# A recurrent attention block and a SoLU feed-forward block on one core: the slot's work put in order of TensorE's tile form

## The chip, the cores and the metric

One core of a Trainium2 chip runs the whole program. The time is that of one execution on the device, in microseconds; for the kernel before, three runs gave 583.88, 577.79 and 580.46, median 580.46. TensorE (PE) multiplies matrices, VectorE (DVE), ScalarE (ACT) and GpSimd (POOL) work elementwise, SyncE (SP) issues transfers. Each takes its own instructions in order. TensorE writes only to PSUM, which here is split into four pairs of banks, named A, B, C and h; whatever stands in a pair must be read out before the next product goes there.

## The reference

For four batches and eight heads of width 40, over 768 tokens, a state S (40 by 40) is carried along; all is float32:

```
y[t] = r[t] . S
Sa   = S . a[t]
S    = S * w[t] - outer(Sa, b[t]) + outer(v[t], k[t])
```

The outputs of the heads, side by side, are x, 3072 tokens of 320. The weights w_in (320 by 1024) and w_out (1024 by 320) come as float64. The second block is

```
h    = x @ w_in
solu = h * softmax(h)
ln   = (solu - mean) / sqrt(var + 1e-6) * g
out  = ln @ w_out
```

## The kernel before

**Tiling.** A chunk is 64 tokens of two batches, so there are 24 chunks (i = 0 to 23), and chunk i carries on the state that chunk i-2 left. Within a chunk the recurrence is written as products of 64 by 64: logs of w are added up by a triangular product (`decay`, L337: pcum), the exponentials scale a, b, k, and r. Everything is transposed on TensorE with an identity (`turned`, L358: a, b, ei, k, v, r and the state) and copied out. `norm` (L424) forms the products of a and b; their lower triangles, 32 by 32, go to DRAM (nt_dram), come back for two chunks at once as blk, one matrix to a partition, and `invert` (L456) inverts them on VectorE in 30 steps of two instructions each (prod, uu; L469 and L471). The inverse goes to DRAM (uu_dram) and `bring` (L481) loads it as tu and uh. `flip` (L494) transposes tu on VectorE; `couple` (py) and `close` (pz) build the 64 by 64 inverse from the parts; a copy by ScalarE follows each (wy, nt, tu).

**A chunk's path.** `scores` (L571) gives ps, masked by VectorE to psi and lv; `carried` and `driven` (L589, L605) add up px from the state and from psi, which ScalarE copies as x0; `solved` (L617) gives pu, out of which come lu's two parts; `read` (L632) gives pyo; `leave` (L646) adds the state's share on VectorE (tot), multiplies on GpSimd by the decays to x and the next state, and SP and POOL queues move x to xT; `stated` and `stated_r` (L551, L559) turn the state and read it with r (pst, psr).

**The second block.** `hidden` (L689) multiplies xT by w_in: contraction 320 = 128 + 128 + 64, the last part with 64-row tiles; `highest`, `exped`, `weighed`, `spreadof` (L701 to L737) are maximum on VectorE, exponential on ScalarE, product on VectorE, square and its sum on ScalarE (written into h's PSUM pair, as a place to throw it), and a power on GpSimd. `folded` (L739) transposes the result to lnT, `output` (L752) multiplies by w_out in two halves of four, and ScalarE scales and copies to osb.

**Weights.** The float64 words are loaded in 13 parts (`land`, L156) and made float32 ("narrowing", `split`, L180) by VectorE and ScalarE in three pieces, begun, scaled and finished. When a part is finished, the next part's load may be issued on the POOL queue.

**Order.** The loop at L863 runs over slots i = -1 to 27, and the order in which calls stand there is the order on every engine; nothing is moved by a scheduler. With LAG = 1, a slot does the recurrence of chunk i, prepares a, b and decays of chunk i+5 and k, v, r of chunk i+2, runs softmax and layer norm of chunk i-3 and the output of chunk i-4. A string for each slot (`plans`, L853) says at six places how many inverse steps VectorE takes there (a number) and where a part of the weights is begun, scaled or finished (b, s, f). From slot 5 on there are two strings, for odd and even slots.

Of the kernel before, what the change touches and what calls it, by code (L numbers as in the profile page):

```python
# [24 lines left out]
LAG = 1  # L25
# [25 lines left out]
def kernel(  # L51
# [32 lines left out]
    small = ctx.enter_context(tc.tile_pool(name="small", bufs=3))  # L84
# [33 lines left out]
    a_t = zeroed(nc.vector, "a", [P, H, C], 4, pad)  # L118
    ei_t = zeroed(nc.vector, "ei", [P, H, C], 1, pad)
    ex_t = [const.tile([P, 2, 4, C + 1], FP32, name=f"ex{n}") for n in range(AHEAD + 2)]  # L120
# [102 lines left out]
    def vector(plan, kept=0):  # L223

        for word in plan.split():
            if word in "bsf":
                dict(b=begin_narrow, s=scale_narrow, f=end_narrow)[word]()
            else:
                some(int(word), kept)

    def turn_g():
        pg = pair("B", "pg")[:, 0]
        nc.tensor.transpose(out=pg[:, 0:NF], in_=g_rows, identity=ident[0:NF, 0:NF])
        for x, y in zip(g_cols, (0, -20, -36)):
            nc.scalar.mul(out=x, in_=pg[:, 0:NF], mul=2.0 ** y)
# [6 lines left out]
    def mean_of(lo, hi, begun, tag):  # L242
        t = pair(tag, "pmean")[:, 0]
        nc.tensor.matmul(t[:, 0:DM], lhsT=ident, rhs=begun, start=True, stop=False)
        mean_part(t, lo, hi, False)
        return mean_kept(t)
# [59 lines left out]
    def load_keys(i, names, queue=nc.sync):  # L306
        if not ok(i):
            return
        for n, ap in (("w", w), ("b", b), ("a", a), ("k", k)):
            if n in names:  # L310
                x = a_t[i % 4] if n == "a" else two.tile([P, H, D], FP32, tag="raw_" + n, name="raw_" + n,
                                                             bufs=3)
# [3 lines left out]
    def load_values(i):  # L316
# [4 lines left out]
        d["raw_r"] = two.tile([P, H, D], FP32, tag="raw_r", name="raw_r")  # L321
        load(d["lv"][:, :, C:], v, i)
        load(d["raw_r"], r, i, nc.gpsimd)
# [13 lines left out]
    def decay(i):  # L337
        if not ok(i):
            return
# [3 lines left out]
        t = (pair("B", "pcum")[:, 0] if i > 9 else h_pair("pcum"))[:, 0:DM]  # L343
        nc.tensor.matmul(t, lhsT=c_("cum"), rhs=d["lw"], start=True, stop=True)  # L344
        nc.scalar.activation(out=ei_t[0][:, :, 0:D], in_=heads(t), func=AF.Exp)
        inv = d["inv"] = two.tile([P, DM], FP32, tag="inv", name="inv", bufs=4)
        nc.scalar.activation(out=inv, in_=t, func=AF.Exp, scale=-1.0)  # L347
# [28 lines left out]
    def decay_turned(i, t=None, y=0):  # L376
# [3 lines left out]
        ex = st[i]["ex"] = ex_t[i % (AHEAD + 2)]  # L380
# [37 lines left out]
    def shared_pair(i):  # L418

        if i not in shared:  # L420
            shared[i] = pair("A", "py")
        return shared[i]

    def norm(i, first=lambda: None):  # L424
# [15 lines left out]
        queue = nc.sync if 1 < i < 4 else nc.gpsimd  # L440
        for x in range(2):
            for e in range(2):
                home = C * x + Q * e
                queue.dma_start(out=blocks[n][e].rearrange("(a x h) s c -> a x s h c", a=GRP, x=2)[at, x],  # L444
# [68 lines left out]
    def close(i):  # L513
# [3 lines left out]
        t = pair("B" if i < 4 else "A", "pz")  # L517
        for u in in_turn(lambda p, q, g, h: (p, p ^ h)):
            p, q, g, h = u
            j = 2 * q + g  # L520
            mm(t[half(p ^ h), p, j * Q:j * Q + Q], wy[half(p), h, j], d["uh"][half(p), H * (p ^ h) + 4 * p + j])
        nc.scalar.copy(out=d["tu"].rearrange("p (h j) c -> p h j c", h=2)[:, :, :, 2 * Q:],
                       in_=t[:, :, 0:4 * Q].rearrange("p h (j c) -> p h j c", j=4))
# [14 lines left out]
    def attend_r(i, tag):  # L538
        if not ok(i):
            return lambda: None  # L540
        t = turned(pair(tag, "pr"), 0, r_t[0])
# [17 lines left out]
    def stated_r(i):  # L559
# [4 lines left out]
        t = pair("C", "psr")  # L564
# [6 lines left out]
    def scores(i):  # L571
# [3 lines left out]
        t = pair("B", "ps")  # L575
# [13 lines left out]
    def carried(i):  # L589
# [5 lines left out]
        d["px"] = pair("C", "px")  # L595
# [9 lines left out]
    def driven(i):  # L605
        if not ok(i):
            return
# [7 lines left out]
        nc.scalar.mul(out=x0, in_=d["px"].rearrange("p h (j d) -> p h j d", j=4)[:, :, :, 0:W2], mul=-1.0)  # L615

    def solved(i):  # L617

        if not ok(i):
            return  # L620
# [9 lines left out]
        nc.scalar.copy(out=o[:, :, :, C:], in_=y[:, :, :, C:])  # L630
# [15 lines left out]
    def leave(i):  # L646
        if not ok(i):
            return
# [9 lines left out]
        else:  # L658
            nc.vector.tensor_copy(out=by_b(tot), in_=y)
        x = two.tile([P, 4, P], FP32, tag="x", name="x", bufs=1)  # L660
        ex = d["ex"][0:W2]
        by_q = lambda x, q: x[0:W2, q::2].rearrange("p (b g) c -> p b g c", b=2)
        for q in range(2):
            nc.gpsimd.tensor_tensor(out=x[0:W2, 2 * q:2 * q + 2].rearrange("p g (b t) -> p b g t", b=2),  # L664
                                    in0=by_q(tot, q)[:, :, :, 0:C], in1=ex[:, :, 2 * q:2 * q + 2, 0:C], op=ALU.mult)
        d["x"] = x
        xT = d["xT"] = two.tile([P, NK, P], FP32, tag="xT", name="xT", bufs=3)
# [3 lines left out]
        if ci == NCH - 1:  # L671
            return
        for q in range(2):
            nc.gpsimd.tensor_tensor(out=by_q(state_of(i)[:, 1], q)[:, :, :, 0:D], in0=by_q(tot, q)[:, :, :, C:],
                                    in1=ex[:, :, 2 * q:2 * q + 2, C:].to_broadcast([W2, 2, 2, D]), op=ALU.mult)
# [13 lines left out]
    def hidden(i, some):  # L689
# [4 lines left out]
        for kt, x in some:  # L694
            if (kt, x) == (0, 0):
                d["h"] = h_pair("h")
            part = slice(0, P) if kt < 2 else half(x)
            mm(d["h"][:, 512 * x:512 * x + 512], d["xT"][part, kt], w_in[part, 2 * kt + (x if kt < 2 else 0)],
               start=(kt, x) in ((0, 0), (NK - 1, 1)), stop=(kt, x) in ((NK - 1, 0), (1, 1)))
# [25 lines left out]
    def spreadof(i):  # L725
# [9 lines left out]
        nc.scalar.activation(out=d["h"], in_=d["e"], func=AF.Square, scale=-float(DFF), bias=d["mu"], accum_out=sq)  # L735
# [3 lines left out]
    def folded(i):  # L739
# [4 lines left out]
        t = pair("A", "plnT")  # L744
# [7 lines left out]
    def output(i, x):  # L752
# [4 lines left out]
        if x == 0:  # L757
            d["out"] = pair("B", "po")[:, 0, 0:DM]
        t = d["out"]
        for f in range(x * NF // 2, x * NF // 2 + NF // 2):  # L760
            nc.tensor.matmul(t, lhsT=d["lnT"][:, f, :], rhs=w2[:, f, :], start=f == 0, stop=f == NF - 1)  # L761
        if x == 0:
            return
# [9 lines left out]
    def some(n, kept=0):  # L773
        while len(steps) > kept and n:
            if next(steps[0], steps) is steps:
# [6 lines left out]
    def begin_inverse(n):  # L782
        steps.append(invert(n))
        next(steps[-1])
# [11 lines left out]
    decay(0)  # L796
    logged(1)
    decay_turned(0)()
    for i in range(4):
# [6 lines left out]
        decay(i + 1)  # L806
# [6 lines left out]
        if i == 1:  # L813
# [8 lines left out]
            load_values(0)  # L822
            load_keys(1, "k")
# [144 lines left out]
```

## Time and profile before

| | before |
|---|---|
| runs, us | 577.79, 580.46, 583.88 |
| span of the profiled execution, us | 580.2 |
| PE, PE weight load busy | 510.6 (88%), 360.5 (62%) |
| DVE, ACT, POOL busy | 407.9 (70%), 316.9 (55%), 299.8 (52%) |
| granted TensorE clock, mean | 0.93 |
| start of pu of chunk 0, 5, 6, 18, 23 | 63.7, 179.4, 199.0, 434.8, 529.2 |
| the chain that ended last | PE 65%, DVE 17%, DMA 9% |

The profile is of one execution, whose own time is its span; it lies 0.2 us under the median. Busy shares are means over stages that have different bounds, so the stages are read by themselves. A product of float32 appears as two instructions. The length that a row gives for a TensorE group contains the time that the last product needs to come out, during which the next group already runs; the distance from one group's start to the next start is what it costs. pu's start marks a slot's beginning in the order before; after the change pu stands late in its slot, and by then the output of chunk i-4, the rest of h, and transposes of this slot have been done, about 8.5 us of TensorE that come later before the change.

### The profile page before, as it was taken

How to read it: one execution, taken by the hardware profiler on the slowest of the kernel's cores; microseconds unless marked ns; L12 is line 12 of the kernel's file. 1: busy time of each engine (PE TensorE's matmuls, PEld its weight loads, DVE VectorE, ACT ScalarE, POOL GpSimd, SP SyncE). 2: the span in 40 equal slices, each digit the busy share in tenths (PEclk: the TensorE clock that was granted, in tenths of full speed). 3: DMA queues.
4: the chain of work that ended last, by engine and by line, in shares of the span. 5: the costliest groups of instructions: out<-in, count | busy, mean ns of one | idle time of the engine just before them, and what ended most of it. 6: DMA issues, size and time to landing. Idle time of an engine off the chain costs nothing.

```text
span 580.2 us, 25261 instructions
## 1 busy us (share of the span) xinstructions
PE 510.6 (88%) x10773; PEld 360.5 (62%) x10773; DVE 407.9 (70%) x1072; ACT 316.9 (55%) x618; POOL 299.8 (52%) x534
## 2 busy tenths in 40 slices
PE   4462764876989999999999999999999989999995
PEld 3241653654766777677667767777777657666543
DVE  4698986996894886877959869779688487332121
ACT  4633573755646565756566566656564455444533
POOL 4554484555635736648576467475773554233200
PEclk9656787879779999999999999999999989999999
DMA  7896886746605536637555475365431431311110
GB/s 152 151 155 135 175 183 114 148 94 113 112 16 124 111 74 134 118 63 141 103 104 114 90 143 113 65 137 105 99 77 39 106 74 32 62 33 27 27 24 23
DMA packets 188200, 56.71 MB, mean 98 GB/s; under 512 B 171680, under 2 KB 181512, under 8 KB 188088
## 3 DMA queue, kind: packets, MB, share of 16 engines
q1 hardware_dynamic: 173288, 36.98, 34.6%
q0 software_dynamic: 12368, 17.19, 12.9%
q8 instruction: 85, 1.39, 1.0%
q10 hardware_dynamic: 2432, 0.92, 0.8%
q14 instruction: 27, 0.22, 0.1%
HBM read 40.10 MB, written 10.22 MB: 87 GB/s over the span
## 4 chain that ended last, share of the span: by engine, by line
PE 65%; DVE 17%; DMA 9%; issue 3%; ACT 3%; SPq 2%; POOL 1%; ACTq 0%; DVEq 0%; POOLq 0%
PE h L276 19%; PE po L761 15%; PE px L276 5%; DVE uu L471 5%; DVE prod L469 5%; PE pyo L276 4%; DMA uu_dram<-uu 3%; PE py L276 3%; PE ps L276 3%; PE pu L276 3%; PE pz L276 2%; PE pkv L363 2%; DMA tu<-uu_dram 2%; PE plnT L747 2%; PE psr L276 2%
## 5 line engine op out<-in xcount | busy, mean ns | idle before, releaser
L276 PE MATMUL h<-w_in,xT 128*128 128x512 f32 (+1 forms) x288 | 123.6, 632 | 0.3
L761 PE MATMUL po<-w,lnT 128*128 128x320 f32 x384 | 118.2, 454 | 1.8 <-ACT lnT L750 1.8
L471 DVE TENSOR_TENSOR uu<-uu,prod 128x30 f32<-128x30 f32 (+4 forms) x360 | 106.2, 295 | 12.4
L469 DVE TENSOR_TENSOR prod<-blk,uu 128x30 f32<-128x30 f32 (+4 forms) x360 | 105.5, 293 | 11.4 <-POOL kb L356 0.7
L664 POOL TENSOR_TENSOR x<-tot,ex 104x256 f32<-104x256 f32 x48 | 32.3, 690 | 130.3 <-DVE tot L656 119.5
L761 PEld LDWEIGHTS po<-w,lnT 128*128 128x128 f32 x384 | 71.3, 194 | 31.9 <-issue 3.2
L444 POOL DMA_DIRECT2D nt_dram<-nt x88 | 52.3, 602 | 24.3 <-ACT c L734 21.4
L276 PEld LDWEIGHTS h<-w_in,xT 128*128 128x128 f32 (+1 forms) x288 | 40.4, 190 | 34.3 <-issue 29.1
L706 DVE TENSOR_REDUCE nmax<-h 128x1 f32<-128x1024 f32 x24 | 29.4, 1224 | 38.0 <-PE h L276 37.5
L510 ACT ACTIVATE wy<-py,cst 128x256 f32<-128x256 f32 x24 | 11.4, 474 | 79.0 <-PE py L276 79.0
L403 DVE TENSOR_TENSOR lu<-pu,cst 128x512 f32<-128x512 f32 x24 | 16.5, 688 | 51.6 <-PE pu L276 51.6
L686 POOL DMA_DIRECT2D xT<-x x96 | 48.7, 511 | 1.2 <-DMA blk<-nt_dram 1.2
L276 PE MATMUL py<-tu,nt 64*64 64x32 f32 x768 | 16.5, 226 | 28.0 <-DVE tot L656 11.6
L714 ACT ACTIVATE e<-h,nmax 128x1024 f32<-128x1024 f32 x24 | 26.8, 1117 | 20.4 <-DVE nmax L706 20.3
L299 POOL DMA_DIRECT2D raw_r<-in_r_dram x48 | 33.8, 707 | 1.4 <-issue 1.3
L276 PEld LDWEIGHTS py<-tu,nt 64*64 64x64 f32 x768 | 15.6, 145 | 30.3 <-issue 19.8
L344 PE MATMUL pcum<-lw,cst 128*128 128x320 f32 x48 | 21.7, 538 | 14.4 <-ACT lw L335 14.4
L737 POOL TENSOR_TENSOR rs<-var,mhalf 128x1 f32<-128x1 f32 x24 | 13.6, 567 | 39.5 <-ACT var L736 38.8
L356 POOL TENSOR_TENSOR kb<-raw_b,inv 128x320 f32<-128x320 f32 x24 | 21.1, 880 | 21.1 <-ACT inv L347 6.9
L722 DVE SCALAR_TENSOR_TENSOR e<-h,e 128x1024 f32<-128x1024 f32 x24 | 29.2, 1215 | 3.8 <-ACT e L714 3.8
L276 PEld LDWEIGHTS pu<-x,tu 64*64 64x64 f32 x768 | 19.5, 142 | 16.8 <-ACT kvT L536 13.7
L735 ACT ACTIVATE h<-e,mu 128x1024 f32<-128x1024 f32 x24 | 26.8, 1116 | 4.1 <-DVE e L722 4.1
(131 smaller groups left out, 1068.9 us busy)
## 6 DMA issues: line engine op xcount, KB each, us to landing
blk<-nt_dram POOLq DMA_DIRECT2D x22, 256.0 KB, 3.7
raw_w<-in_w_dram SPq DMA_DIRECT2D x48, 80.0 KB
a<-in_a_dram SPq DMA_DIRECT2D x48, 80.0 KB
raw_r<-in_r_dram POOLq DMA_DIRECT2D x48, 80.0 KB, 3.5
lv<-in_v_dram SPq DMA_DIRECT2D x48, 80.0 KB
out_dram<-osb SPq DMA_DIRECT2D x47, 80.0 KB
raw_b<-in_b_dram SPq DMA_DIRECT2D x44, 80.0 KB
raw_k<-in_k_dram SPq DMA_DIRECT2D x42, 80.0 KB
```

Source lines behind the costliest of these rows:

```text
L276: nc.tensor.matmul(o, lhsT=lhsT, rhs=rhs, start=start, stop=stop, skip_group_check=True)
L299: queue.dma_start(out=x[half(p), :, 0:D], in_=ap[2 * bp + p, :, ci * C:(ci + 1) * C, :].rearrange("h t d -> t h d"))
L444: queue.dma_start(out=blocks[n][e].rearrange("(a x h) s c -> a x s h c", a=GRP, x=2)[at, x], in_=nt[home:home + Q].rearrange("p h j c -> p ...
L469: nc.vector.tensor_tensor(out=t, in0=nb[:, j:j + 1, j + 1:Q].to_broadcast([P, n_c, m]), in1=u[:, 0:n_c, j:j + 1].to_broadcast([P, n_c, m]) ...
L471: nc.vector.tensor_tensor(out=u[:, 0:n_c, j + 1:Q], in0=u[:, 0:n_c, j + 1:Q], in1=t, op=ALU.subtract)
L664: nc.gpsimd.tensor_tensor(out=x[0:W2, 2 * q:2 * q + 2].rearrange("p g (b t) -> p b g t", b=2), in0=by_q(tot, q)[:, :, :, 0:C], in1=ex[:, : ...
L686: nc.gpsimd.dma_start(out=xT[to:to + Q, 2], in_=x[at + P - 3 * D:at + D, 2])
L706: nc.vector.tensor_reduce(out=nmax, in_=d["h"], axis=AX.X, op=ALU.max, negate=True)
L714: nc.scalar.activation(out=e, in_=d["h"], func=AF.Exp, bias=d["nmax"], accum_out=d["esum"])
L722: nc.vector.scalar_tensor_tensor(out=d["e"], in0=d["h"], scalar=1.0 / DFF, in1=d["e"], op0=ALU.mult, op1=ALU.mult, accum_out=d["mu"])
L735: nc.scalar.activation(out=d["h"], in_=d["e"], func=AF.Square, scale=-float(DFF), bias=d["mu"], accum_out=sq)
L761: nc.tensor.matmul(t, lhsT=d["lnT"][:, f, :], rhs=w2[:, f, :], start=f == 0, stop=f == NF - 1)
```

## The change

- **TensorE's order.** A slot now begins with all transposes (ei, b, k, v in pairs C and B; a and r in pair A), h's 64-row products, lnT's and the state's transposes; then h's 128-row products, the decay sum and the output, unbroken; then pu, psr, ps, px from the state, py (both), pyo, pz, px from psi. k, v and r are turned for chunk i+1, not i+2, and the scores of chunk 0 go from the prologue to slot -1.
- **PSUM.** h is in pair C, psr, px, lnT's transposes and the thrown-away square in pair h, ps in C, po, py and pz in B. All eight output products stand in one place.
- **Evictions** of px (x0) and the leaving of chunk i (state first, then x) are done at the start of slot i+1; lu's copy comes after psr's.
- **x and state** are multiplied by VectorE, no longer by GpSimd.
- **Transfers.** nt goes out by SP and POOL, one half each; loads of r come at the slot's start, of v at its end, of b, a, k behind those of tu and uh. Buffers: a 3 for 4, raw w 2 for 3, ex 8 for 7, xT 4 for 3, the small pool 2 for 3.
- **Plans.** Narrowing is dealt anew over slots -1 to 3; "o" before a number means inverse steps of the older pair only, and what is left of a pair that is due is done before it is brought.
- With LAG = 3 softmax still belongs to chunk i-3 and the output to chunk i-4, and the last slot is 27.

```diff
-LAG = 1
+LAG = 3
...
-    def vector(plan, kept=0):
+    def vector(plan):
...
-                some(int(word), kept)
+                some(int(word.strip("o")), (i + 2) // GRP if "o" in word else N)
...
-            shared[i] = pair("A", "py")
+            shared[i] = pair("B" if i >= 0 else "A", "py")
...
-        queue = nc.sync if 1 < i < 4 else nc.gpsimd
         for x in range(2):
             for e in range(2):
                 home = C * x + Q * e
+                queue = (nc.sync, nc.gpsimd)[e] if i > 3 else nc.sync if 1 < i else nc.gpsimd
...
-        t = pair("C", "psr")
+        t = pair("h", "psr")
...
-        t = pair("B", "ps")
+        t = pair("C", "ps")
...
-        d["px"] = pair("C", "px")
+        d["px"] = pair("h", "px")
...
+        for q in range(2 * (ci < NCH - 1)):
+            nc.vector.tensor_tensor(out=by_q(state_of(i)[:, 1], q)[:, :, :, 0:D], in0=by_q(tot, q)[:, :, :, C:],
+                                    in1=ex[:, :, 2 * q:2 * q + 2, C:].to_broadcast([W2, 2, 2, D]), op=ALU.mult)
         for q in range(2):
-            nc.gpsimd.tensor_tensor(out=x[0:W2, 2 * q:2 * q + 2].rearrange("p g (b t) -> p b g t", b=2),
+            nc.vector.tensor_tensor(out=x[0:W2, 2 * q:2 * q + 2].rearrange("p g (b t) -> p b g t", b=2),
                                     in0=by_q(tot, q)[:, :, :, 0:C], in1=ex[:, :, 2 * q:2 * q + 2, 0:C], op=ALU.mult)
...
-        nc.scalar.activation(out=d["h"], in_=d["e"], func=AF.Square, scale=-float(DFF), bias=d["mu"], accum_out=sq)
+        nc.scalar.activation(out=pair("h", "sq").rearrange("p a b -> p (a b)"), in_=d["e"], func=AF.Square, scale=-float(DFF), bias=d["mu"], accum_out=sq)
...
+        -1: ("", "10", "", "", "b s 4", "2 f"),
+        0: ("", "b s 5 f b s 4 f", "", "", "b s o3", "f"),
+        1: ("", "b s o5 b s f 3 f", "", "", "b s 4", "1 f"),
+        2: ("", "b s 4 b s 4 f 1 b s f", "", "2 f", "o4", "o2"),
+        3: ("", "o6", "2", "b s", "5 f", "2"),
+        4: ("", "7", "2", "3", "o4", "o2"),
...
+    for i in range(-1, N + LAG + 1):
+        j, c = i + AHEAD, i - LAG
+        plan = plans.get(i, ("", "o5 1", "2", "2", "3", "2") if i % GRP else ("", "7", "2", "2", "o3", "o2"))
+        if i >= 0:
+            load_keys(j + 3, "w")
+        load_r(i + 3)
...
+        vector(plan[0])
+        td = pair("C", "pa")
+        ei_out, b_out = decay_turned(j + 1, td, 0), front_b(j, td, 1)
+        kv_out = attend_kv(i + 1)
+        ta = pair("A", "pb")
+        front_out, r_out = front(j, ta, 0), attend_r(i + 1, ta, 1)
+        hidden(c, ((2, 0), (2, 1)))
+        for evict in (front_out, leave_out, ei_out, b_out, x_out, r_out):
+            evict()
...
+        ln_out = folded(c - 1)
+        kv_out()
+        ln_out()
+        if ok(i + 1) and i + 1 >= NPAIR:
+            stated(i + 1, pair("A", "pst"), 0)()
+        left(i - 1)
+
+        hidden(c, ((0, 0), (1, 0), (0, 1), (1, 1)))
+        by_value(i + 2)
...
+        decay(j + 2, pair("A", "pcum")[:, 0])()
+        tb = pair("B", "po")
+        vector(plan[1])
+        if i >= 1:
+            some(Q, (i + 1) // GRP)
+            bring(i + 1)
+        load_keys(j + 2, "bak")
...
+        highest(c)
+        exped(c)
+        vector(plan[2])
+        weighed(c)
+        spreadof(c)
+        scaled(j + 1)
+        output(c - 1, tb[:, 0])
...
+        vector(plan[3])
+
+        split_lu = solved(i)
         stated_r(i + 1)
+        split_lu()
+        mask_values = scores(i + 1)
         flip(i + 1)
+        mask_values()
         carried(i + 1)
+        norm(j, lambda: couple(i + 1)())
         if ok(j) and j % GRP == GRP - 1:
             begin_inverse(j // GRP)
+        read(i)
+        if i >= 0:
+            load_values(i + 3)
+        if ok(j + 3) and i >= 0:
+            logged(j + 3)
         close(i + 1)
+        x_out = driven(i + 1)
+        vector(plan[4])
+        leave_out = summed(i)
         vector(plan[5])
```

## The prediction

> **What bounds the kernel now.** I read the page's slices first, then busy time by stage, then TensorE's timeline of one slot, and last VectorE's and GpSimd's timelines of that slot. The first two, on the page and in the stages I chose, show three regimes.
>
> ```profile
> PE   4462764876989999999999999999999989999995
> DVE  4698986996894886877959869779688487332121
> PEclk9656787879779999999999999999999989999999
> ...
> 51.00:175.00 124.00, 89.17 (x2138) 69.14 (x2139) 104.29 (x280) 66.15 (x135) 67.56 (x111) 0.79 0.60 120
> 175.00:199.00 24.00, 24.00 (x558) 16.95 (x550) 15.87 (x40) 15.77 (x30) 15.53 (x26) 1.00 0.60 121
> 199.00:435.00 236.00, 235.40 (x5455) 168.31 (x5458) 186.28 (x495) 144.79 (x286) 145.55 (x254) 1.00 0.54 105
> ```
>
> In the stage lines the columns are PE, PEld, DVE, ACT, POOL busy, then clock. From 199 to 435 us TensorE is busy 235.4 of 236 at full clock: TensorE is the bound, and only less TensorE time helps. From 51 to 175 us VectorE is the bound (104.3 of 124; weights are narrowed and inverses begun), and TensorE's clock is 0.79. The end (529 to 580) is TensorE with its softmax waits.
>
> TensorE's timeline gives the slot (start, length, operation); one slot is 337.32 - 317.71 = 19.61 us, and the same in nearly all of the twelve from 199 on.
>
> ```profile
> 317.71 0.94 PE L276 MATMUL pu<-x,tu 64*64 64x104 f32 x32
> ...
> 318.94 0.65 PE L276 MATMUL ps<-rT,kvT 40*64 40x64 f32 x32
> 319.52 1.13 PE L276 MATMUL h<-w_in,xT 64*128 64x512 f32 x4
> ...
> 324.44 0.90 PE L276 MATMUL pyo<-lv,kb 64*64 64x104 f32 x32
> 325.15 0.89 PE L276 MATMUL pyo<-lu,kb 64*64 64x104 f32 x32
> 325.98 2.42 PE L761 MATMUL po<-w,lnT 128*128 128x320 f32 x8
> 328.33 1.10 PE L276 MATMUL px<-st,aT 40*64 40x128 f32 x32
> ```
>
> The reader is to see starts, not lengths. The two ps groups are 32 alike: the first takes 0.47 us to the next start, the second 0.58, because h after it has another tile form. The pyo groups are twins too: 0.71 to the next pyo, 0.83 to po. Every change of form (64*64, 64*128 or 64*104, 128*128) costs 0.10 to 0.12 us.
>
> **The change, part by part.** *Fewer form changes.* Today a slot changes form ten times: ps to h, ei to h, pcum to psr, pyo to po, po to px, py to po, po to pz, px to pkv, pr to h, h to pu. Afterwards three are left. Seven fewer at 0.105 are 0.73 us: 19.61 becomes 18.88 if nothing waits. The count of products does not change.
>
> *What stands in the way of that.* Today po and h, 2.35 and 1.9 us long, lie between the dependent small products and cover every eviction. In the new order I walk the slot from its first transpose (t=0) with today's distances: transposes to 1.4, h's 64-row pair to 2.4, folded and state transposes to 3.3, h to 7.0, pcum to 7.6, output to 12.2, small products to 18.9. Waits on the way:
> - h's first pair takes the PSUM pair of ei and b transposes, which ScalarE empties with two copies at 0.48 us each; the second is done at about 1.55, so TensorE waits 0.15. Nothing covers that.
> - x's copy is third in that queue (done 2.3), before the folded transposes at 2.5: hidden.
> - nmax (1.14), e (1.2), weighed (1.2) and the square (1.3) run one after another after h ends at 7.0, to 12.0; psr, which now takes the pair that the square writes, starts at 12.9. Margin 0.9.
> - in the odd slots VectorE must begin the next inverse before nmax, and its input goes nt, DRAM, blk: now from the nt copy (17.4) to the blk issue took 5.5 us with four issues on POOL; with two queues about 4.3, plus 3.7 to land: t=6.6 to 7.5 in the next slot, and the first step is 1.2 long. nmax then starts at 7.8 to 8.7 instead of 7.1, and psr is 0 to 0.8 late. I take 0.3 per odd slot, 0.15 per slot.
> - psr's copy (0.59), then px from the state: margin 0.1. psi, flip, lv on VectorE, then couple's py: margin 0.1. wy's copy before pz: 0.7. The A pair of pyo, freed by the sum on VectorE at the slot's end, before a's transposes: 0.9.
> Sum: 18.88 + 0.15 + 0.15 = 19.18, a gain of 0.43 per slot. With all margins kept it would be 0.73; with each thin one missed, below zero.
>
> *x and state on VectorE.* These rows show what moves, and what GpSimd does to VectorE meanwhile:
>
> ```profile
> 308.73 1.33 POOL L664 TENSOR_TENSOR x<-tot,ex 104x256 f32<-104x256 f32 x2 [4.16 <-DVE tot L656]
> 310.02 0.88 POOL L674 TENSOR_TENSOR st<-tot,ex 104x160 f32<-104x160 f32 x2
> ...
> 315.99 0.28 DVE L471 TENSOR_TENSOR uu<-uu,prod 128x114 f32<-128x114 f32 x1
> 316.30 1.11 DVE L469 TENSOR_TENSOR prod<-blk,uu 128x126 f32<-128x126 f32 x1
> 317.44 0.84 DVE L471 TENSOR_TENSOR uu<-uu,prod 128x126 f32<-128x126 f32 x1
> ```
>
> No VectorE row has these shapes. Its own products from SBUF take 0.41 us for 320 columns without a predecessor and 0.33 for 128 with one, so two of 256 and two of 160 take 1.2 to 1.6; I take 1.4. VectorE has 33.1 us of work in two slots now (15.5 and 17.6 between idle times); with 2.8 more, and some 1.5 less stretching by GpSimd (the 1.11 beside 0.28 stands beside a kb product), 34.4 of 38.4: it fits, but the margins above are thin because of it. GpSimd becomes freer; that earns nothing by itself.
>
> *Steady stage.* Thirteen slots from the sixth to the eighteenth: 13 x 0.43 = -5.6. *Later slots*, five, 18.9, 22.6, 17.9, 17.9, 17.1 long: 5 x 0.43 = -2.2, and of the 22.6 some 4.4 are one wait of py (2.78) with the half clock after it, because flip came late behind the trip of an inverse through DRAM. That trip now starts at about t=6 of an odd slot, clear of blk, with 9 us to go; in eight trips it took 7 to 11 us. I take -3, with ends +2 and -4.4.
> *End.* The period of the last blocks is 10.05 us; h no longer waits for the square of the block before (its own pair): 9.76, three times -0.3, and po's last wait of 1.79 shrinks by 0.5: -1.4.
>
> *Before 175 us.* VectorE's queue, each instruction at the pitch of undisturbed rows, adds to 101 us between 51 and 175; it stood idle 12.7 (two waits of flip for tu, 4.51 and 4.19, are most), so 10.3 is stretching. The five slots get 5 x 1.4 = +7.0; a little under half of the stretching goes with GpSimd's products, -4.6; one of the two flip waits should go since the inverse is now finished first in the slot, -4.4. Narrowing is only dealt anew: 13 parts before and after, each at 1.9 to 2.6. Scores and k/v transposes of the first block leave the prologue for slot -1, where the first flip has to wait anyway. Together -2. Ends: both flip waits gone and little stretching, -12; idle at sums and at nmax while TensorE is at half clock, +8.
>
> **Sum**: -5.6 - 2.2 - 3 - 1.4 - 2 = -14.2. The span is 580.2 and the median 580.46, so nothing lies around it that matters: **566 us**.
>
> **The rivals.**
> *VectorE becomes the bound* (0.17). For it: 34.4 of busy, plus the waits it cannot fill (psi for ps 0.8, e 0.2, sum 0.2, a's transposes 0.2, blk's 1 in odd slots), is 38.2 of 38.4; if the stretching stays at 3.2, two slots need 39.2, 19.6 each. Against: kb would now run while VectorE reads PSUM (lu, psi, lv), and rows of that kind beside kb kept 0.69. Steady gain gone: 580.2 - 2 - 3 - 1.4 = 574.
> *The row of small products stalls* (0.15; the slower side). Its place is the chain psr, state copy, px and psi, flip, py, where po used to stand between. If osb (0.5) stands before the state copy, VectorE's steps overrun psi by 0.6, and flip's data come 1 us late in odd slots, a slot waits 1.6 instead of 0.3: 566 + 18 x 1.3 = 589. It decides from 0.73 of waiting per slot on. For it: two of the margins are 0.1. Against: they are computed from distances that repeat within 0.01.
> *The clock falls in every slot* (0.06). Idle of 1.84 us before py at 168.16 made the next eight po take 4.63 instead of 2.42. The new slot has 2.2 us of transposes within its first 3.3. If these did not count as work, a drop per slot at 1.7 us would give 566 + 18 x 1.7 = 597. Against: from 62.0 to 63.7 TensorE did transposes alone, and the clock rose to full at 65.7 all the same. The Trainium skill, page "TensorE: Matmul & The Clock Gate", section "PE-mode transpose", says that transposes do not count as busy for the clock gate as other products do; by that rule this rival would be the likely one, and the rows so far speak against it.
> *The prologue gains its full 12* (0.12): 566 - 10 = 556, and with all margins kept, 13 x 0.3 less, 552.
>
> **Numbers.** Forecast 0.50. Under 1% this kernel can hardly be told from no change: 574.7 to 586.3. Faster: 0.48 of the forecast, 0.12, half of the first rival: 0.68. Same: 0.02 and the other half, and a little of the stalls: 0.13. Slower: 0.19. The range takes in the full prologue gain and the stalls, not the clock: 549 to 592.
>
> **What would show it.** Right: pu to pu at 19.0 to 19.4 in the steady stage, three short steps of 0.1 between forms, no PE wait over 0.5. VectorE's busy in that stage at 0.88 or more. Wrong: repeated PE waits for st, flip or psi; nmax waiting long behind uu's first step; a clock under 1.00 after 200 us; pu of the sixth slot (now at 179.4, then with 8.5 us more work before it) later than 190.

## The result and the profile after

Four runs of the changed kernel gave 600.46 to 604.46 us, median 600.82; four of the kernel before beside them had a median of 581.62. The ratio is 1.035, 95% interval 1.030 to 1.040: **slower by 3.5%**, where 566 us had been forecast (range 549 to 592). The profiled execution after spans 598.9 us, 18.7 more than before (580.2). The span of an execution lies some 2 us under its time here (598.9 for 601.08), so the 580.2 belongs to a time of some 582, and a forecast of 566 that starts from it is one of the span.

First the page of the kernel after: its slices, TensorE's instruction packets, and the chain that ended last.

```profile
PE   4544554858999889999997989999899899999995
...
DVE  4798677886786676876866766866768678534321
...
PEclk9996668869799999999999999999999999999999
...
q8 instruction: 85, 1.39, 1.0%
...
PE 64%; DVE 12%; issue 7%; ACT 7%; DMA 6%; SPq 2%; POOL 1%; ACTq 0%; DVEq 0%; POOLq 0%
```

The digit 9 that TensorE had from a third of the span on is broken by 7s and 8s, the granted clock stays full behind the eleventh slice, and the chain has 7% of "issue", time in which an engine waited for nothing that the profile shows; before it had 3%. The q8 line gives number, MB and share: 85 packets carry 1.39 MB, 16 KB each. TensorE has 10773 products and 10773 weight loads, so a packet holds some 256 of its instructions, 64 bytes each.

Then busy time by stage (PE, PEld, DVE, ACT, POOL, and the clock behind them):

```profile
51.00:175.00 124.00, 84.92 (x2002) 69.76 (x1998) 97.53 (x273) 66.11 (x135) 45.61 (x75) 0.75 0.60 118
199.00:435.00 236.00, 214.58 (x5129) 162.23 (x5131) 168.38 (x505) 134.77 (x267) 97.46 (x168) 1.00 0.52 100
```

From 199 to 435 us TensorE is busy 214.6 of 236, where it was 235.4; VectorE has 168 where it had 186. Neither is the bound any more. What TensorE waits for in that stage (us in total, times, longest):

```profile
PE py L275 <- issue: 9.1, 9, 1.7
PE pyo L275 <- issue: 4.6, 6, 1.2
PE px L275 <- issue: 2.2, 3, 1.0
PE h L275 <- ACT bT L379: 1.9, 7, 0.3
PE pkv L369 <- issue: 1.2, 2, 0.8
PE pb L369 <- issue: 0.9, 1, 0.9
PE pa L369 <- issue: 0.8, 1, 0.8
```

In the same stage the kernel before had one wait, for VectorE:

```profile
PE py L276 <- DVE tot L656: 0.5, 1, 0.5
```

After, 22 waits of 18.7 us in sum end without any semaphore. One slot of TensorE's timeline shows where they fall:

```profile
237.14 0.94 PE L275 MATMUL pu<-x,tu 64*64 64x104 f32 x32
237.91 0.64 PE L275 MATMUL psr<-rT,s 40*64 40x64 f32 x32
...
240.65 0.66 PE L275 MATMUL py<-tu,nt 64*64 64x32 f32 x31
241.78 0.24 PE L275 MATMUL py<-tu,nt 64*64 64x32 f32 x1 [0.47 <-issue]
241.79 0.98 PE L275 MATMUL pyo<-lv,kb 64*64 64x104 f32 x32
...
243.70 0.96 PE L275 MATMUL px<-lv,psi 64*64 64x104 f32 x30
245.15 0.34 PE L275 MATMUL px<-lv,psi 64*64 64x104 f32 x2 [0.49 <-issue]
...
247.24 1.20 PE L275 MATMUL h<-w_in,xT 64*128 64x512 f32 x4 [0.27 <-ACT bT L379]
```

They stop in the middle of a group: 31 products, a pause, one more. The 32 read the same two tiles, so a late operand would have held the first of them. In the DMA records each of the 22 waits ends 1.2 to 1.5 us after a packet of q8 has landed.

The 18.7 us of the span by stage, with 8.5 us of work moved ahead of pu as forecast:

| stage | before | after | difference | forecast |
|---|---|---|---|---|
| up to pu of the sixth slot | 179.4 + 8.5 | 194.1 | +6.2 | -2 |
| 13 steady slots | 255.4 | 271.2 | +15.8 | -5.6 |
| five later slots | 94.3 | 89.7 | -4.7 | -5.2 |
| end | 51.1 - 8.5 | 44.0 | +1.4 | -1.4 |

Of the 271.2, 19.6 are issue waits; the remaining 251.6 are close to the forecast's 249.8.

Of three kernels below (half the output inside, two groups inside, before with x and state on VectorE) the profiled execution was slower than the runs compared, so of their profiles the waits and busy shares are used, and no stage times.

### The profile page after: what moved, and what is told of

Read it like the earlier page. It is cut to its first block, busy times and chain, and to the rows that moved or that the text cites. A ratio compares the mean times of both kernels' runs of the same rounds, so it can differ in the third digit from the quotient of the medians.

```text
span 598.9 us, 25310 instructions
## 1 busy us (share of the span) xinstructions
PE 498.4 (83%) x10773; PEld 370.4 (62%) x10773; DVE 404.5 (68%) x1164; ACT 317.2 (53%) x618; POOL 224.2 (37%) x402
## 3 DMA queue, kind: packets, MB, share of 16 engines
q8 instruction: 85, 1.39, 1.0%
## 4 chain that ended last, share of the span: by engine, by line
PE 64%; DVE 12%; issue 7%; ACT 7%; DMA 6%; SPq 2%; POOL 1%; ACTq 0%; DVEq 0%; POOLq 0%
PE h L275 17%; PE po L768 14%; PE py L275 7%; PE pyo L275 7%; PE px L275 5%; PE ps L275 3%; PE pu L275 2%; DVE prod L475 2%; DVE uu L477 2%; PE pcum L347 2%; PE plnT L756 2%; PE psr L275 2%; PE pa L369 1%; DMA blk<-nt_dram 1%; ACT ex L388 1%
## 5 line engine op out<-in xcount | busy, mean ns | idle before, releaser
L768 PE MATMUL po<-w,lnT 128*128 128x320 f32 x384 | 107.4, 433 | 1.1 <-ACT lnT L759 1.1
L475 DVE TENSOR_TENSOR prod<-blk,uu 128x30 f32<-128x30 f32 (+4 forms) x360 | 92.9, 258 | 11.5 <-DMA blk<-nt_dram 3.0
L477 DVE TENSOR_TENSOR uu<-uu,prod 128x30 f32<-128x30 f32 (+4 forms) x360 | 91.7, 255 | 12.4
L450 POOL DMA_DIRECT2D nt_dram<-nt x48 | 30.0, 629 | 64.8 <-ACT nt L442 64.8
L693 POOL DMA_DIRECT2D xT<-x x48 | 25.5, 531 | 66.9 <-DVE prod L475 34.3
L695 POOL DMA_DIRECT2D xT<-x x96 | 48.6, 511 | 1.1 <-DMA blk<-nt_dram 1.0
L662 DVE TENSOR_TENSOR tot<-pyo,st 104x512 f32<-104x512 f32 (+1 forms) x44 | 23.9, 586 | 26.0 <-PE pyo L275 25.8
L744 ACT ACTIVATE sq<-e,mu 128x1024 f32<-128x1024 f32 x24 | 26.8, 1118 | 23.6 <-DVE e L731 23.6
L275 PE MATMUL px<-st,aT 40*64 40x128 f32 x704 | 25.9, 286 | 6.3 <-ACT st L575 6.2
L347 PEld LDWEIGHTS pcum<-lw,cst 128*128 128x128 f32 x48 | 9.9, 230 | 33.9 <-ACT lw L338 21.4
L275 PE MATMUL pyo<-lv,kb 64*64 64x104 f32 x768 | 27.4, 275 | 4.1 <-issue 2.9
```

What stands on the lines that cost most here:

```text
L275: nc.tensor.matmul(o, lhsT=lhsT, rhs=rhs, start=start, stop=stop, skip_group_check=True)
L475: nc.vector.tensor_tensor(out=t, in0=nb[:, j:j + 1, j + 1:Q].to_broadcast([P, n_c, m]), in1=u[:, 0:n_c, j:j + 1].to_broadcast([P, n_c, m]) ...
L477: nc.vector.tensor_tensor(out=u[:, 0:n_c, j + 1:Q], in0=u[:, 0:n_c, j + 1:Q], in1=t, op=ALU.subtract)
L695: nc.gpsimd.dma_start(out=xT[to:to + Q, 2], in_=x[at + P - 3 * D:at + D, 2])
L744: nc.scalar.activation(out=pair("h", "sq").rearrange("p a b -> p (a b)"), in_=d["e"], func=AF.Square, scale=-float(DFF), bias=d["mu"], acc ...
```

## The experiments

Theory A: TensorE's instructions come in at some 256 per 3.7 us, and the row puts 704 of them (11 groups of 32 products, each with its weight load) into some 6.8 us. Rivals: VectorE's share, the dependences inside the row, and that the products or the order themselves cost this.

**The supply by itself.** To the kernel before, independent small products on constants are added at the end, which nothing waits for:

```diff
+    for n, tag in ((64, "A"), (104, "B"), (104, "C"), (64, "h")):
+        t = psum.tile([P, 2, 512], FP32, tag=tag, name=f"run{n}")
+        for _ in range(12):
+            nc.tensor.matmul(t[:, 0, 0:DM], lhsT=ident, rhs=cst[:, 0:DM], start=True, stop=True)
+        for _ in range(36 if n == 64 else 28):
...
+                mm(t[half(p), q, at:at + n], ident[half(q), half(q)], cst[half(q), 0:n])
```

> The kernel before with four runs of independent 64-row products on constants behind its end: 576 of 64 columns, 448 of 104, 448 of 104, 576 of 64, twelve 128-row products of 320 columns ahead of each (transfers are nearly silent then). Undisturbed, a group of 16 products takes 0.466 (64 columns) or 0.716 us (104), so the runs would be 16.8 and 20.0 us. Theory A: after the first few hundred instructions they stop again and again; four groups are a block of 256 instructions, and a block takes the same time, 3.3 to 4 us, at both widths: runs of 30 and 24 us or so. If instructions are always there in time: 16.8 and 20.0, no waits.

TensorE's timeline at the end of that kernel:

```profile
582.04 3.02 PE L276 MATMUL run<-cst 64*64 64x64 f32 x188
586.35 2.09 PE L276 MATMUL run<-cst 64*64 64x64 f32 x128 [1.30 <-issue]
590.09 2.09 PE L276 MATMUL run<-cst 64*64 64x64 f32 x128 [1.65 <-issue]
...
620.14 6.88 PE L276 MATMUL run<-cst 64*64 64x104 f32 x292
627.68 3.08 PE L276 MATMUL run<-cst 64*64 64x104 f32 x128 [0.66 <-issue]
631.43 3.08 PE L276 MATMUL run<-cst 64*64 64x104 f32 x128 [0.66 <-issue]
```

After a first piece of 188 to 396 products come pieces of exactly 128, 256 instructions, one packet. They start 3.5 to 4.0 us apart, mostly 3.74, at either width: the narrow ones are done in 2.1 us and wait 1.65, the wide ones take 3.1 and wait 0.66. The limit is on instructions, 14.6 ns each (3.74 us / 256), not on the work that they give. The four runs take 31.4, 24.5, 24.3 and 31.8 us, as theory A had it (30 and 24). The first piece is what was stored, with what arrived meanwhile. A packet's own transfer takes 0.9 to 1.7 us in the records, here and in after, and no two overlap; what fills the rest of the 3.74 us is not shown.

**The same columns from fewer instructions.** After, but in eight of the eleven groups every second product is left out and its neighbour is twice as wide (so every second result uses its neighbour's weights):

```diff
-        for u in in_turn(lambda p, q, g, h: (p ^ h, p)):
+        for u in in_turn(lambda p, q, g, h: (p ^ h, p), two_of(2)):
...
-            mm(t[half(p), h, at:at + W2], d["tu"][x, 4 * p + 2 * q + g, Q:], x0[x, h, 2 * q + g])
+            mm(t[half(p), h, at:at + 2 * W2], d["tu"][x, 4 * p + 2 * q + g, Q:], x0[x, h, 2 * q:2 * q + 2])
```

> After, with the same order, tile forms, columns and waits, but in eight of the eleven groups of the row (both ps, psr, py of a and b, px of psi, pu, both pyo) every second product is left out and the one before it is twice as wide (64x64 becomes 64x128, 64x104 becomes 64x208): TensorE streams the same number of columns from half the instructions, 448 instead of 704 in the row. What is computed is so changed: every second product uses the weights of its neighbour. Theory A (TensorE is limited by the supply of 256 instructions per 3.7 us): issue waits from 199 to 435 us of 0 to 3 us instead of 18.7, the 13 steady slots 249 to 256 us instead of 271, time 576 to 587. Rival B (the waits belong to the order or to the products themselves, not to the number of instructions): issue waits of 15 to 20, steady slots 268 to 275, time 597 to 606.

Ratio 0.9955 (0.991 to 0.9999), median 580.91. TensorE's waits of that kernel from 199 to 435 us, that stage's busy times, and starts of its timeline:

```profile
PE psr L278 <- ACT sq L747: 3.7, 5, 1.1
PE h L278 <- ACT bT L382: 3.3, 12, 0.3
PE px L278 <- issue: 0.2, 1, 0.2
```

```profile
199.00:435.00 236.00, 228.74 (x3998) 164.82 (x3991) 184.36 (x556) 149.19 (x291) 108.31 (x187) 1.00 0.57 107
```

```profile
251.21 0.93 PE L278 MATMUL pu<-x,tu 64*64 64x208 f32 x16
251.97 0.62 PE L278 MATMUL psr<-rT,s 40*64 40x128 f32 x16
...
269.97 0.94 PE L278 MATMUL pu<-x,tu 64*64 64x208 f32 x16
```

The groups keep their length (pu 0.76 us to the next start, 0.77 in after), the order of the groups is unchanged, and the issue waits are gone: 18.7 us became 0.2. The 13 slots take 249.7 us; one in which psr does not wait takes 18.76 (251.21 to 269.97). The weight loads are halved with the products, but they are not the limit: out of the store, in the run before, a product with its load takes 16 ns. The two runs together show theory A: the instructions alone made the steady stage slow.

**Breaking the row.** If the supply is the limit, work of few instructions inside the row should shorten the waits. First two idle products of 128 by 320, on constants, between couple's py and pyo:

```diff
+        if i > 4 and ok(i + 1):
+            idle = pair("C", "idle")[:, 0]
+            for _ in range(2):
+                nc.tensor.matmul(idle[:, 0:DM], lhsT=ident, rhs=cst[:, 0:DM], start=True, stop=True)
```

> The changed kernel with two 128-row products of 320 columns more in each slot from the sixth on, placed in the row of small products between couple's py and pyo, on constants and into a PSUM pair that nobody reads; they take 1.1 us of TensorE and two more form changes, 0.2, with only 8 instructions. Theory A: instructions are brought meanwhile, so the unexplained waits behind them shrink by about as much: a slot 0 to 0.5 us longer, 600 to 610. Theory B, or any cause that is not the supply of instructions: 18 slots x 1.3 longer, 624.

Ratio 1.057 (1.050 to 1.064). The issue waits fell from 18.7 to 9.8 us, and the steady slots rose by 8.0 us, 0.62 a slot; the five later slots, with few issue waits, rose by 6.6, 1.3 a slot. The same work costs half where it stands beside an issue wait. The time, 615.8, lies between the two theories' figures.

Then half of the output is put inside the row, and scores ahead of psr:

```diff
-        output(c - 1, tb[:, 0])
+        halves = 4 <= i < N
+        output(c - 1, tb[:, 0], 0, NF // 2 if halves else NF)
...
+        mask_values = scores(i + 1)
         stated_r(i + 1)
         split_lu()
-        mask_values = scores(i + 1)
+        if halves:
+            output(c - 1, tb[:, 0], NF // 2)
```

> After, with the row of small products broken: in slots 4 to 23 the second half of the output (8 records, 2.3 us) stands between the scores and the flip's products, and psr behind the scores; two more changes of form a slot (0.2 us). Theory A (TensorE's instructions come at about 256 per 3.7 us, so 704 of them in 6.8 us empty what is stored): now some 256 and some 448 of them stand apart by 2.3 us of few instructions, so the issue waits from 199 to 435 us fall from 18.7 to 6 or less, a slot of the steady stage takes 19.4 to 20.0 us instead of 20.9, and the time is 583 to 592. Rival B (the waits come with the number of instructions in a slot, about 898, wherever they stand): issue waits stay at 15 to 19, and with the two changes of form the time is 600 to 606.

TensorE's waits from 199 to 435 us in that kernel:

```profile
PE ps L275 <- DVE prod L475: 7.0, 5, 2.3
PE ps L275 <- DVE e L731: 3.5, 5, 1.0
PE px L275 <- issue: 3.0, 3, 1.2
```

Issue waits are 5.5 us in all, as A said, but the time missed: ratio 1.060 (1.051 to 1.069). With 2.3 us of output gone from ahead of the row, ps comes before VectorE has done with h, whose pair it takes: a wait of some 1 us a slot that I had not counted. So the whole output inside, below, does worse still.

> As the run with half the output inside the row, but all of the output (16 records, 4.5 us) stands there, and none ahead of the row; the first part of the row then follows h and the decay product directly. Theory A: 4.5 us of few instructions in the middle let a whole block of 256 arrive, but before the row there are only h's 3.7 us; issue waits from 199 to 435 us of 2 to 9, time 585 to 596. Rival B: issue waits of 15 to 19, time 599 to 606. Besides, the square (ScalarE, done about 5 us after h) now ends behind the start of psr: up to 1 us a slot of waits of psr for sq are possible under both.

One time, 692.7 us. Issue waits 1.9 us, and 28 us of waits for the softmax and for pcum's eviction took their place. These waits alone do not make up the 92 us against after: TensorE's clock was 0.89 in that stage. Both theories missed the time. The run shows what else the output in front of the row does: it covers the softmax.

A smaller step, pu alone or pu and psr between the output's halves (in the second with the square back in h's own pair, and a new dealing of the narrowing):

> After, with pu alone (64 of the 704 instructions of the row) put between the two halves of the output; everything else as in after, two more changes of form a slot. Theory A: 64 instructions fewer in the unbroken row are worth up to 0.93 us of waiting a slot: issue waits from 199 to 435 us of 6 to 11 instead of 18.7, the 13 steady slots 264 to 268 instead of 271. Rival B: 17 to 20 and 271 to 275. The stage before the sixth slot as in after (pu at 193 to 195).

> After, with pu and psr (128 of the 704 instructions of the row) put between the two halves of the output, where each half gives TensorE 2.2 us of few instructions; for that the square goes back into h's own pair, so psr no longer waits for it. Two more changes of form a slot (0.2 us). Besides, the narrowing of slots 0 to 3 is dealt as in the run before it, but without the part that stood ahead of nmax in slot 3. Theory A (256 instructions per 3.7 us): the row of 576 and the 96 transposes behind it fit into what is stored and arrives, so issue waits from 199 to 435 us are 0 to 6 us, the 13 steady slots take 253 to 260 us instead of 271. Rival B (waits come with the 898 instructions of a slot, wherever): 15 to 20 us of issue waits, 270 to 275. For the stage before: if the wait of psr (5.65) in slot 3 of the last dealing was due to that one part, pu of the sixth slot comes at 185 to 190; if the row's own chain gives the time back elsewhere, at 192 to 196. Time under A 580 to 590, under B 594 to 604.

With pu alone nothing changed: 18.4 us of issue waits, 275.3 for the steady slots, 607.2 in one run. These are rival B's figures, not A's. With both the issue waits are 14.2 and the ratio is 1.022 (1.011 to 1.032), an estimate of some 8 us less than after; that too is far from A's range and near B's, and of the three things changed in it only the dealing was run by itself (below). B as it stands cannot hold either: the kernel before has as many instructions in a slot of 19.61 us, and no such wait.

My count of A was too simple: it took the store as full when the row begins. In the packet records of after a new packet starts to load when some 0.4 to 1.2 packets are left (an estimate, counted from where the waits begin), and only one is under way at a time. By this a row that begins with little left waits however long it rested before; no run tests that by itself. The first wait of a slot begins behind some 340 to 570 of the row's instructions, 1.3 to 2.2 packets. Fewer instructions in the dense stretch help for sure only where the stretch is shorter than what may be left plus what arrives.

**The row in the order before.** Before, with both output halves in one run ahead of psr:

```diff
         decay(j + 2)
+        output(m - 3, 0)
+        output(m - 3, 1)
         stated_r(i + 1)
...
-        output(m - 3, 0)
-
         leave(i)
...
         spreadof(m - 2)
-        output(m - 3, 1)
```

> The kernel before with one edit: both halves of the output stand in one run ahead of psr, so that psr, both pyo, both px, both py, pz and the transposes behind them (about 230 small products) follow each other unbroken, as in the changed kernel; x and state stay on GpSimd, all else stays. Theory A (TensorE works through its instructions in a dense row faster than they are brought; a block of 16 KB is brought at a time): TensorE waits that no semaphore explains, near none in this kernel now, come to 0.7 to 1.5 us in each slot, each ending some 1.4 us after an instruction packet has landed; four form changes less (-0.42), wy's copy no longer covered (+0.6), so a slot of 20.3 to 21.0 for 19.61 and a time of 592 to 605. Theory B (the loss comes from x and state on VectorE and the handovers that go with it): no such waits, a slot of 19.3 to 19.9, 576 to 587.

Ratio 1.124 (1.116 to 1.132). TensorE's waits from 199 to 435 us:

```profile
PE pz L276 <- ACT nt L436: 11.7, 11, 1.1
PE po L761 <- ACT inv L347: 8.6, 10, 0.9
PE py L276 <- DVE tot L656: 4.6, 10, 0.5
...
PE px L276 <- issue: 0.3, 1, 0.3
```

Both theories missed: the row never ran unbroken, since each group waited for an eviction that the output's halves had covered. As a test of the supply it failed; it shows that in the old order the halves were a cover for evictions, too.

**x and state on VectorE.** The part alone, on the kernel before (the diff), and, on the kernel after, its half undone: x alone back on GpSimd.

```diff
-            nc.gpsimd.tensor_tensor(out=x[0:W2, 2 * q:2 * q + 2].rearrange("p g (b t) -> p b g t", b=2),
+            nc.vector.tensor_tensor(out=x[0:W2, 2 * q:2 * q + 2].rearrange("p g (b t) -> p b g t", b=2),
...
-            nc.gpsimd.tensor_tensor(out=by_q(state_of(i)[:, 1], q)[:, :, :, 0:D], in0=by_q(tot, q)[:, :, :, C:],
+            nc.vector.tensor_tensor(out=by_q(state_of(i)[:, 1], q)[:, :, :, 0:D], in0=by_q(tot, q)[:, :, :, C:],
```

> Before, with x and state computed by VectorE instead of GpSimd and nothing else changed: one part of the change alone. Theory A (the row of small products costs the time of the change; where x and state are computed is a gain or nothing): 572 to 584 us, no issue waits of TensorE from 199 to 435 us. Rival B (VectorE with x and state in its queue makes after slower): 590 to 604, VectorE at 0.85 or more of the steady stage, and waits of TensorE for VectorE's results there.

> The changed kernel with x's two products back on GpSimd, state's two stay on VectorE (0.8 us less of VectorE per slot). Theory A: the unexplained waits in 199 to 435 us stay at about 19 us, the steady slot at 20.4 to 21.4; the time within 595 to 603, the gain if any before 190 us, where VectorE has little idle. Theory B: the slot falls by 0.8 or more, 585 or less.

On the kernel before, VectorE costs time: ratio 1.014 (1.007 to 1.020), 589.9 us, between A's range and B's edge; no issue waits to speak of (0.2), as A said. On the kernel after, x back on GpSimd costs more: 1.057 (1.051 to 1.063), 615.6 us, outside the range of either theory, with the issue waits unchanged at 19.0, as A said. So in the new order x on VectorE is a gain of some 15 us (estimate from the two medians), in the old order it and state are a loss of 8. VectorE, busy 0.79 and 0.71 of the steady stage, is the bound in neither. Why GpSimd costs so much in the new order is not settled: 3.8 us of the 13.8 in its span came before the sixth slot, 4.7 in the steady slots, 5.6 in the five later ones, and the end was 0.3 shorter.

**Before the sixth slot.** There after's TensorE waited 12.8 us for the flip (tu), so narrowing was moved behind the flip in VectorE's queue, twice:

```profile
PE py L275 <- DVE tu L504: 12.8, 4, 7.0
```

> After, with the narrowing of weights dealt anew in the slots 0 to 3: fewer parts ahead of lu, psi and flip in VectorE's queue, more behind lv, and each part's scaling by ScalarE put further ahead of VectorE's use of it. Nothing else changes. Theory P (what was lost before the sixth slot is VectorE's narrowing standing between TensorE's row and the flip it waits for, 12.8 us of waits of py for tu there): pu of the sixth slot at 184 to 190 instead of 194.1, time 590 to 597. Rival Q (the loss is in the row's own chain, flip to pyo to sum to the next slot's transposes, whatever narrowing stands where): pu of the sixth slot at 193 to 197, time 599 to 604. The issue waits after 199 us stay as they were under both.

> After, with only the narrowing of slots 0 to 3 dealt as in the run with pu and psr inside the output; nothing else changes. Theory P (the dealing of the change cost time before the sixth slot): pu of the sixth slot at 188 to 191 instead of 194.1, and the time 3 to 6 us under after's: 594 to 599. Rival Q (the earlier pu there came from the order of psr and the square): 193 to 196, time 599 to 604. Issue waits from 199 to 435 us as in after, 17 to 21 us, under both.

The second dealing:

```diff
-        0: ("", "b s 5 f b s 4 f", "", "", "b s o3", "f"),
-        1: ("", "b s o5 b s f 3 f", "", "", "b s 4", "1 f"),
-        2: ("", "b s 4 b s 4 f 1 b s f", "", "2 f", "o4", "o2"),
-        3: ("", "o6", "2", "b s", "5 f", "2"),
+        0: ("", "b s 9 f", "", "", "b s o3", "f b s"),
+        1: ("", "o5 3 f", "", "b s", "4 f b s", "1 f"),
+        2: ("", "b s 8 1 f", "", "b s 2", "o4 f b s", "o2 f"),
+        3: ("", "b s o6", "2", "b s", "5 f f", "2"),
```

The first had pu of the sixth slot at 192.8 and 604.0 us in one run, the second at 192.0 and ratio 1.042 (1.037 to 1.047), no better than after's 1.035. TensorE's waits of the second dealing from 50 to 194 us:

```profile
PE pst L369 <- ACT rT L379: 8.0, 3, 5.5
PE pcum L347 <- DVE uu L477: 7.6, 1, 7.6
...
PE py L275 <- DVE tu L504: 1.0, 2, 0.7
```

The flip's waits fell from 12.8 to 1.0 us, and that of pst for rT grew from 3.2 to 8.0. From the first pu to the sixth the two dealings took 118.8 and 117.0 us, after 122.0 (119.7 in the run with the idle products, which has the same instructions up to there), but their first pu came 1.9 and 2.9 us later. So the dealing did not bring back the 6.2. What I had overlooked stands earlier. TensorE's rows around the first pu, before and then after:

```profile
63.68 1.66 PE L276 MATMUL pu<-x,tu 64*64 64x104 f32 x32
...
67.80 0.81 PE L344 MATMUL pcum<-lw,cst 128*128 128x320 f32 x2
```

```profile
69.77 1.43 PE L347 MATMUL pcum<-lw,cst 128*128 128x320 f32 x2 [6.56 <-ACT lw L338]
72.06 1.66 PE L275 MATMUL pu<-x,tu 64*64 64x104 f32 x32 [0.85 <-ACT inv L352]
```

In the new order the decay sum (pcum) stands ahead of pu, and in the first slot it waits 6.6 us for the logarithm of w, which ScalarE takes behind copies that wait themselves. So pu of chunk 0 is 8.4 us late. The five slots behind it took 122.0 us for 115.7, but one more chunk's h and output, some 8 us, fall into them; by this estimate they lost nothing. In the two dealings the decay sum waits 7.9 and 7.6 us there. No run puts the decay sum behind pu, so what this wait is worth is argued from the timeline, not shown.

**The later slots.** Last, on the kernel before, only the second queue for nt:

```diff
-        queue = nc.sync if 1 < i < 4 else nc.gpsimd
...
+                queue = (nc.sync, nc.gpsimd)[e] if i > 3 else nc.sync if 1 < i else nc.gpsimd
```

> Before, with only the way of nt through DRAM changed as the change has it: from the fifth block on its four transfers go over two queues (SP and POOL) instead of POOL's alone. Theory L1 (the 4.7 us that the change gained in the last slots come from the shorter trip of an inverse, which made flip late in one slot of 22.6 us): that slot falls to 18 to 20 us, steady slots stay at 19.6, time 576 to 580, ratio 0.992 to 0.998. Rival L2 (they come from where the trip starts and ends in the new order of the slot, not from the queues): the long slot stays at 22 to 23 us and the time within 0.3% of before.

Ratio 1.003 (0.999 to 1.007), as rival L2 said, and the long slot stays, 22.4 us, with its wait:

```profile
PE py L276 <- DVE tot L656: 2.7, 1, 2.7
```

So the queues alone do not bring the 4.7 us gained there; they come with the new order of the slot. No kernel that computes the reference was faster than before.

## Why the prediction was wrong

**The step that failed** is "19.61 becomes 18.88 if nothing waits. The count of products does not change": the supply of instructions was put at nothing, and neither the list of waits behind it nor a rival had it. I counted the products, but not how many instructions fall into a stretch. Before, output and h stood between the small products, and the some 900 instructions of a slot (21546 in 24) were spread over 19.61 us, 21.8 ns each. After, 704 stand in 6.8 us, 9.7 ns each, where 14.6 can be had. No row of before showed a single wait of the kind. The rival "the row of small products stalls" named the place and a slower time, 589, but by luck: its reason was the chain of psr, psi and flip, and no wait for these is among those of the steady stage.

**What was right.** The chain of semaphores held: no wait for st, flip or psi in the steady stage, 0.27 us for bT instead of 0.15, the square once for 0.6. With the supply out of the way, in the run of double width, the 13 slots took 249.7 us; 13 x 19.18 are 249.3. That the two are so close is in part luck. In that run the waits for bT and for the square add to 8.1 us, 0.62 a slot where I had 0.30; without them a slot takes 18.57 instead of 18.88, of which some 0.2 is its shorter row.

**VectorE.** I gave two slots 34.4 us where before needs 33.1, and both count the short gaps between its instructions. By that measure two slots of after (257.55 to 298.97) need 31.9, 30.0 of busy and 1.9 of such gaps. x and state cost 1.13 a slot instead of 1.4, and the stretching by GpSimd, of which I had left half, is mostly gone: over the whole run a prod takes 258 ns in the mean for 293, a uu 255 for 295. After's VectorE timeline:

```profile
267.31 0.55 DVE L675 TENSOR_TENSOR st<-tot,ex 104x160 f32<-104x160 f32 x2
267.77 0.75 DVE L678 TENSOR_TENSOR x<-tot,ex 104x256 f32<-104x256 f32 x2
268.44 0.21 DVE L475 TENSOR_TENSOR prod<-blk,uu 128x56 f32<-128x56 f32 x1
```

From 267.31 to 268.44 both are done. My sign of 0.88 of VectorE's time mixed two measures: the busy share leaves the gaps out, and by it before has 0.79, after 0.71 and the run of double width 0.78. The first rival fell with it.

**The clock.** It stays at 1.00 in the steady stage, with 2.2 us of transposes in each slot. The Trainium skill, page "TensorE: Matmul & The Clock Gate", section "PE-mode transpose", has transposes not count as busy in the same way; in this amount, between other products, no drop is seen here.

**Before the sixth slot** I had -2, with ends of -12 and +8; the profile has +6.2. VectorE's terms did not fail: from pu of the first slot to pu of the sixth it is busy 94.2 us for 94.3, with x and state in it, and its waits of flip for tu's transfer, the term -4.4, fell from 9.4 to 1.1 (50 to 181 us before, 50 to 194 after). But between the two pu it stood idle 27.9 us for 21.4, since it now waits 6.5 for ScalarE's scaled weights and 15.3 for TensorE's products (3.4 before). And no term stood for TensorE waiting ahead of the first pu, 6.6 us for the decay sum's input.

```profile
DVE tu L498 <- DMA tu<-uu_dram: 9.4, 3, 4.5
```

```profile
DVE bits L200 <- ACT scale L192: 6.5, 4, 2.5
...
DVE tu L504 <- DMA tu<-uu_dram: 1.1, 1, 1.1
```

**Later slots**: -4.7 for -5.2, with luck in the sum. The long slot went from 22.55 to 17.42 us, 5.1 less where I had 3.4; the first of the five became 1.4 longer, with 1.8 us of issue waits; the other three gained 0.2 to 0.4 each. That the trip starts clear of blk, my reason for the long slot, is borne out as far as the queues alone do nothing. **End**: the period of the last blocks fell further than I had it, 10.05 to 9.49 us instead of 9.76, but waits of 1.3 (lu), 0.8 (square) and 1.1 us (lnT) are new or left: +1.4 for -1.4.

## What to carry to other kernels

Before gathering small products into one run, count instructions per microsecond in it, weight loads included: here a stretch denser than one per 14.6 ns ran dry after some 340 to 570 instructions, though no engine, clock or semaphore was at its limit. Work of few instructions between small products is a cover for the supply and for evictions at once; wider products, fewer instructions for the same columns, remove the limit. And a wait taken away in a stage where two engines take turns comes back under another name.

## What the runs showed that was not expected

- TensorE's instructions arrive in packets of 16 KB on q8, one at a time. In a run without end a packet of 256 comes every 3.74 us, 29 ns for a product with its load, at 64 and at 104 columns alike. Out of the store they go much faster: 128 products of 64 columns in 2.09 us, 16 ns each, and 14 ns (0.46 us for 32) in the rows of after. The Trainium skill, page "TensorE: Matmul & The Clock Gate", section "Wait — 56ns, not 53.3ns?", has starts never closer than about 25 ns, without a word on products that fill a part of the array only; for these on quarters of it the rows show 14, and the measurement decides.
- The waits show up as "issue", in the middle of a group of like products. That, and that they end 1.2 to 1.5 us behind a packet, is how they are told from an operand that is late.
- x by GpSimd or VectorE: some 15 us worse on GpSimd in one order, and with state 8 us better there in the other, with neither engine near its limit.
